# A planned attention and gated-MLP kernel on one core: sharing the three-bank set between ScalarE and VectorE, gating the down projection's halves from PSUM, and recounting the last pass's narrow matmuls

## The chip, the core and the metric

The kernel runs on one NeuronCore of one Trainium2 chip. The metric is device time in microseconds (us) of one execution. A core has five engines with instruction queues of their own: TensorE (PE in the profile; its weight loads are PEld), VectorE (DVE), ScalarE (ACT), GpSimd (POOL) and SyncE (SP). The last two mostly issue DMAs here. PE writes its results to PSUM, which has eight banks of 512 fp32 columns by 128 partitions; ACT and DVE read them there.

## What is computed

The input `x` has 2048 rows (S) of 640 (D) in bf16. A branch of attention (32 heads of 20) and a gated MLP (F = 1728) both read the layer-normed rows; the result is `x + attention * silu(MLP)`.

```python
xn = _layernorm(x)
q, k, v = (xn @ wqkv) ...                        # 32 heads of 20
p = softmax(q @ k.T * 20 ** -0.5)
s = (p @ v).reshape(S, D) @ wo
h = sigmoid(xn @ w_gate) * (xn @ w_up)
g = silu(h @ w_down)
out = x + s * g
```

## The kernel before, in words

**Passes.** After a setup (load, layer norm, transposes, first projections) the work is cut into 32 passes: four chunks of 512 queries (`qc`, QC) times eight groups of four heads (`g`). A pass has 64 score banks: 16 key tiles times four heads, each 128 keys by 512 queries, one PSUM bank. `NB` is 32 x 64 = 2048 banks. The four heads of a group lie on four row strips of PE, so their score matmuls run side by side.

**Exponentials.** ACT takes banks in sets: a set of three banks (`sc0`) and a set of two (`sc1`) in turn, one instruction for a whole set (`act_exp`, L1162). VectorE takes single banks by an approximation in four steps over 512 columns (`dve_exp`: L1173, which is the only one to read PSUM, then L1178, L1182, L1186). Its bank is one of the two work banks (`misc0`, `misc1`), taken as a `spare` by `take_bank` where `spare_wanted` holds one back. `issue` plans one round: it takes the next banks in order, scores them, adds the exponential to ACT's queue and, if VectorE's backlog is under 2500 ns and a work bank is free, a further bank for VectorE. A set is scored again when its `Cell` in `sets` says that it was read.

**Probabilities times values.** `pv_batch` and `pv` (L1274) accumulate eight banks at a time into one bank, `oacc`; row 0 of each head's strip sums the probabilities. After a pass `normalise` copies `oacc` to SBUF (L771), sends the sums through DRAM by GpSimd's DMAs (L772 to L788) and multiplies (L800). The last pass is done in two halves of 256 queries, so that the first half can be finished while the second is still in work: each score bank then holds two key tiles of 256 queries. `first_half` (L806 to L815) copies the first half of `oacc`, `half_job` (L817 to L867) spreads the reciprocals of the sums by two sets of narrow fp32 matmuls (L823, four columns out; L844, 128 columns out) and does the last output matmuls (L862) for row tiles 0 and 1. `part_job` (L750) has summed the first six head groups of the last chunk's output before, times the gate, plus `x` by an accumulating GpSimd DMA (L758).

**The gated MLP.** `gateup_job` makes `hT` (tanh on ACT, L650, reading PSUM; product on VectorE, L660). `down_job` makes one row tile of 640 columns in two halves of 320: 14 matmuls (L679) into a work bank, VectorE copies the half to SBUF (L683), and after both halves ACT takes tanh of the 640 columns from SBUF (L690) and VectorE multiplies (L695). For the last chunk the product stays in SBUF (`gq_last`), for the others it goes to DRAM by a GpSimd DMA (L699). `out_job` (L718, L724) multiplies it into the attention output.

**What sets the order.** The order on every engine is written out while the kernel is built, by a planner that keeps a clock for PE (`pe[0]`) and one each for ACT and VectorE. Its `Engine.run` starts the task that can start first, and by rank among equals. PE's loop (L1351 on) chooses between a round of scores, a batch of probability matmuls, a step of a `Job`, and a zero matmul. Jobs are sorted by a due bank; the last pass's jobs by `NB - 40`, `NB - 16` and `NB - 12`, and at most two jobs are in flight (`runnable`). `zero_add` (L1250 into `oacc`, L1256 into a free work bank) adds a matmul of zeros whenever the planned streaming time of the last 3400 ns (`streamed`, `WINDOW`) is under 2500 (`ENOUGH`). Each matmul enters that count with its planned time: 136 ns for each pick of L823 and 432 for each matmul of L844.

**The end.** After the loop, remaining jobs are emitted, VectorE copies the second half of `oacc` (L1369), the PSUM pool is closed and opened anew, and the same steps follow for row tiles 2 and 3 without the planner: first parts of the output (L1376), picks (L1383), reciprocal (L1388), spread (L1390), fp32 matmuls (L1392), product (L1394), second parts (L1376), `gated` (L871) and `summed` (L874), which also stores.

Of the kernel before, what the change touches and what calls it, by code (L numbers as in the profile page):

```python
# [15 lines left out]
P = 128  # L16
HEAD = 32
GH = 4
# [26 lines left out]
def kernel(  # L45
# [332 lines left out]

    class Engine:
# [286 lines left out]
    def down_job(tt):  # L666
        c, t4 = divmod(tt, QC // P)
        yield "known", lambda: (bulk[0] == NFT and pe[0] > bulk_t[0] + LANDED and len(h_cells.get(c, [])) == NFT and (tt < 2 or tt - 2 in gq_cells)
                                and (c < NQC - 1 or front() >= PER_PASS * (NG * c + t4 + 1)))
        yield "wait", h_cells[c] + ([gq_cells[tt - 2]] if tt > 1 else [])  # L670
        hT = hTs[c]
        d2 = glu[0].tile([P, D], FP32, tag="d2", bufs=2, name="d2")
        got = []
        for h in range(2):
            e0_, e1_ = h * HALF, (h + 1) * HALF
            held, psd = yield "bank",
            for kf in range(NFT):
                fsz = fsz_list[kf]
                nc.tensor.matmul(psd[:, 0:HALF], lhsT=hT[0:fsz, kf, t4 * P:(t4 + 1) * P],  # L679
                                 rhs=glu[1][0:fsz, kf, e0_:e1_], start=(kf == 0), stop=(kf == NFT - 1))  # L680
                yield "mm", MM3
            got.append(dve.add(400.0, [Cell(pe[0] + PE_OUT)], lambda psd=psd, e0_=e0_, e1_=e1_:
                               nc.vector.tensor_copy(out=d2[:, e0_:e1_], in_=psd[:, 0:HALF]), 1))  # L683
            give_bank(held, got[-1])
        d_cells.setdefault(c, []).append(Cell(pe[0]))
        made = {}

        def tanh():
            made["t"] = glu[0].tile([P, D], BF16, tag="td", bufs=1, name="td")
            nc.scalar.activation(out=made["t"], in_=d2, func=ACT.Tanh, scale=0.25)  # L690

        def finish():
            last = c == NQC - 1
            gq = kT_all[:, t4, :].bitcast(FP32)[:, 0:D] if last else d2
            nc.vector.scalar_tensor_tensor(out=gq, in0=made["t"], scalar=1.0, in1=d2, op0=ALU.add, op1=ALU.mult)  # L695
            if last:
                gq_last[t4] = gq
            else:
                nc.gpsimd.dma_start(out=gq_dram[tt, :, :], in_=d2)  # L699

        turned = act.add(590.0, got + td_free[-1:], tanh, 0, EXP_LAG)
        td_free.append(dve.add(740.0, [turned], finish, 2))
        gq_cells[tt] = td_free[-1]

# [101 lines left out]
    half = {}  # L806

    def first_half(done):
        def copy():
            half["oev"] = glu[0].tile([P, KD, P], BF16, tag="wg", bufs=WB, name="oev")  # L810
            half["oev"] = half["oev"].rearrange("p k f -> p (k f)").bitcast(FP32)[:, 0:QH]
            nc.vector.tensor_copy(out=half["oev"], in_=oacc[:, 0:QH])

        cell = dve.add(340.0, [Cell(done + PE_OUT)], copy, -1)
        half["cell"] = cell  # L815
        return cell

    def half_job():
        n, tiles = QH // P, range(QH // P)
        yield "wait", [half["cell"]]  # L820
        held, pd = yield "bank",
        for t4 in tiles:
            nc.tensor.matmul(pd[:, t4 * GH:(t4 + 1) * GH], lhsT=half["oev"][:, t4 * P:(t4 + 1) * P], rhs=pick,  # L823
                             start=True, stop=True, skip_group_check=True)
            yield "mm", MM3
# [6 lines left out]
        def spread():  # L832
            made["rb"] = glu[0].tile([P, KD, P], BF16, tag="wu", bufs=WB, name="rb")
            made["rb"] = made["rb"].rearrange("p k f -> p (k f)").bitcast(FP32)[:, 0:n * P].rearrange(
# [8 lines left out]
        for t4 in tiles:  # L843
            nc.tensor.matmul(prl[:, t4 * P:(t4 + 1) * P], lhsT=made["rb"][:, t4, :, :].rearrange("p j i -> p (j i)"),  # L844
                             rhs=identf, start=True, stop=True, skip_group_check=True)
            yield "mm", 2 * MM5

        def scale():
            oTs[steps[-1]] = wk.tile([P, QC], BF16, tag="oT", bufs=NG + 3, name="oT")
            nc.vector.tensor_tensor(out=oTs[steps[-1]][:, 0:QH], in0=half["oev"], in1=prl[:, 0:QH], op=ALU.mult)  # L850

        cell = dve.add(340.0, [Cell(pe[0] + PE_OUT)], scale, -1)
# [4 lines left out]
        for t4 in tiles:  # L857
# [9 lines left out]
            dve.add(740.0, [out_cells[(NQC - 1) * 4 + t4], *got], lambda t4=t4: summed(t4, pair[:, t4 % 2 * D:(t4 % 2 + 1) * D]), 2)  # L867
# [12 lines left out]
    LAST, QH = NB - PER_PASS, QC // 2  # L880
# [6 lines left out]
    HALF_COST = 12 * MM3 + 4 * MM5  # L887
# [46 lines left out]
    for t4 in range(4):  # L934
        jobs.append(Job(part_job(t4), PART_COST, len(steps) - 1, NB - (40 if t4 < 2 else 16)))
    jobs.append(Job(half_job(), HALF_COST, len(steps) - 1, NB - 12, when=lambda: half))
# [83 lines left out]
    def runnable(p):  # L1020
        k = 0
        while True:
            if k == len(flight):
                if k == MOST:
# [13 lines left out]
    def fill(p, room=1e18):  # L1038
# [4 lines left out]
        pe_do("fill", took)  # L1043
# [24 lines left out]
    NEEDED, NEEDED_LAST = 6, 12  # L1068
# [36 lines left out]
    def dve_bank(banks):  # L1105
# [3 lines left out]
        ends = LAST + PER_PASS // 2 if LAST <= b < LAST + PER_PASS // 2 else PER_PASS * (b // PER_PASS + 1)  # L1109
# [12 lines left out]
    def unit(b):  # L1122
        return b // PER_PASS if b < LAST else len(steps) - 1 + (b - LAST) // (PER_PASS // 2)

    def pieces(b):
        r = b % PER_PASS
        if b < LAST:
            return [(r // GH, 0, 0, QC)]
        half, r = divmod(r, PER_PASS // 2)
        return [(2 * (r // GH) + k, half * QH, k * QH, QH) for k in range(2)]  # L1130

    def full(p):
        return KT if p < len(steps) - 1 else KT // 2
# [62 lines left out]
    def issue():  # L1196
# [6 lines left out]
        if (ci > 1 and dve.backlog + max(0.0, dve.t - pe[0]) < D_BACKLOG  # L1203
                and all(c.t is not None for c in d_made[-2:-1])):
            extra = dve_bank(taken)
            if extra is not None:
                split = take_bank("spare")
        ps = psum.tile([P, n, 512], FP32, tag=f"sc{ci % 2}", bufs=1, name="sc")
# [3 lines left out]
        sets[ci % 2] = act_exp(ps, taken, begun)  # L1212
# [10 lines left out]
    def pv_batch():  # L1223

        p = pv_pass[0]
        if p > len(steps):
# [37 lines left out]
    def pv(batch):  # L1264
# [3 lines left out]
        for k in range(2):  # L1268
            for part in range(1 if p < len(steps) - 1 else 2):
# [18 lines left out]
        if all(n == most for n in pv_count[0]):  # L1288
# [4 lines left out]
            elif p == len(steps) - 1:  # L1293
                oacc_free[0] = first_half(pe[0])
# [10 lines left out]
    while pv_pass[0] <= len(steps):  # L1305
# [47 lines left out]
        if zero_add(room):  # L1353
            idle = False
            continue
        soon = [q[k][1].made.t for q in ready_p for k in range(min(2, len(q)))]
        times = [until, pe[0] + 150.0] + [t + SEM for t in soon if t is not None]
        pe[0] = min(t for t in times if t > pe[0] + 1.0)

    while flight or jobs or timed or act.queue or dve.queue:  # L1360
# [5 lines left out]
    tiles = range(QH // P, QC // P)  # L1366
    units = [(t4, h) for t4 in tiles for h in range(2)]
    oev = wk.tile([P, QC], FP32, tag="oev", bufs=OBUFS, name="oev")
    nc.vector.tensor_copy(out=oev[:, QH:], in_=oacc[:, QH:])  # L1369
# [3 lines left out]
    banks, pd, prl = banks[1:5], banks[6], banks[7]  # L1373
# [6 lines left out]
    for bank, (t4, h) in zip(banks[:3], units):  # L1380
        out_mm(bank, t4, h, NG - 2)
    for k, t4 in enumerate(tiles):
        nc.tensor.matmul(pd[:, k * GH:(k + 1) * GH], lhsT=oev[:, t4 * P:(t4 + 1) * P], rhs=pick,  # L1383
                         start=True, stop=True, skip_group_check=True)
    out_mm(banks[3], *units[3], NG - 2)
# [5 lines left out]
    for k, t4 in enumerate(tiles):  # L1391
        nc.tensor.matmul(prl[:, t4 * P:(t4 + 1) * P], lhsT=rb[:, k, :, :].rearrange("p j i -> p (j i)"), rhs=identf,  # L1392
                         start=True, stop=True, skip_group_check=True)
    nc.vector.tensor_tensor(out=oTs[qc, g][:, QH:], in0=oev[:, QH:], in1=prl[:, QH:], op=ALU.mult)  # L1394
# [34 lines left out]
```

## Time and profile before

| | |
|---|---|
| runs | 898.45, 894.53, 894.62 us; median 894.62 |
| profiled execution | 898.68 us, of which its span (first to last instruction) is 896.5 |
| busy: PE, DVE, ACT, POOL | 809.1, 838.6, 871.4, 161.6 us |
| exponentials on ACT | 717, busy 828.9 us |
| VectorE's first steps (L1173) | 256, 685 ns each |
| mean granted PE clock | 0.99 |

How to read the profile: one execution is recorded. Busy time is the union of an engine's instructions; the mean of one is given in ns. Instructions of an engine overlap at their ends, so the time that one costs is the distance from its start to the next start. "Idle before" is time in which an engine ran nothing, with the instruction whose end released it. The slices cut the span in 40, a digit is the busy share in tenths, and PEclk is the clock that PE was granted, in tenths of full speed. The chain is the work that ended last, followed back.

### The profile page before, as it was taken

How to read it: one execution, taken by the hardware profiler on the slowest of the kernel's cores; microseconds unless marked ns; L12 is line 12 of the kernel's file. 1: busy time of each engine (PE TensorE's matmuls, PEld its weight loads, DVE VectorE, ACT ScalarE, POOL GpSimd, SP SyncE). 2: the span in 40 equal slices, each digit the busy share in tenths (PEclk: the TensorE clock that was granted, in tenths of full speed). 3: DMA queues.
4: the chain of work that ended last, by engine and by line, in shares of the span. 5: the costliest groups of instructions: out<-in, count | busy, mean ns of one | idle time of the engine just before them, and what ended most of it. 6: DMA issues, size and time to landing. Idle time of an engine off the chain costs nothing.

```text
span 896.5 us, 16915 instructions
## 1 busy us (share of the span) xinstructions
PE 809.1 (90%) x6228; PEld 291.8 (33%) x6311; DVE 838.6 (94%) x1483; ACT 871.4 (97%) x837; POOL 161.6 (18%) x305
## 2 busy tenths in 40 slices
PE   5899899998998999999999998999999888999896
PEld 3344333332223333232233332222332322333342
DVE  7799999999999999997999999999999989999994
ACT  6999999999999999999999999999999999999993
POOL 7401111101111212111111221110121220111120
PEclk9999999999999999999999999999999999999996
DMA  8113231235442234223212342303022432200021
GB/s 316 46 36 89 68 105 35 56 94 150 120 122 41 64 89 71 64 58 79 56 25 79 95 65 65 78 24 79 27 73 64 107 64 67 56 20 14 14 59 45
DMA packets 107672, 64.40 MB, mean 72 GB/s; under 512 B 80350, under 2 KB 101906, under 8 KB 107498
## 3 DMA queue, kind: packets, MB, share of 16 engines
q1 hardware_dynamic: 97382, 47.21, 19.8%
q0 software_dynamic: 10208, 16.11, 8.0%
q8 instruction: 49, 0.80, 0.4%
q14 instruction: 33, 0.27, 0.1%
HBM read 50.45 MB, written 16.13 MB: 74 GB/s over the span
## 4 chain that ended last, share of the span: by engine, by line
ACT 63%; issue 18%; PE 11%; DVE 7%; DMA 1%; SPq 0%; ACTq 0%; DVEq 0%
ACT p L1162 58%; PE sc L1140 4%; ACT tnh L650 3%; PE oacc L1274 2%; DVE dy L1173 1%; PE work L643 1%; PE work L123 1%; DVE du L1178 1%; PE work L679 1%; ACT td L690 1%; DVE stats L226 1%; DVE p L1186 1%; DVE du L1182 1%; PE work L149 1%; DMA x_sb<-in_A_x_dram 0%
## 5 line engine op out<-in xcount | busy, mean ns | idle before, releaser
L1162 ACT ACTIVATE p<-sc 128x1536 bf16<-128x1536 f32 x717 | 828.9, 1361 | 3.4 <-PE oacc L1274 1.4
L1140 PE MATMUL sc<-qT,kT_all 21*128 21x512 bf16 (+1 forms) x1850 | 280.9, 377 | 56.5 <-ACT p L1162 48.5
L1173 DVE TENSOR_SCALAR dy<-spare 128x512 f32<-128x512 f32 x256 | 175.2, 685 | 22.6 <-PE spare L1140 20.0
L1140 PEld LDWEIGHTS <-kT_all 21*128 21x128 bf16 x2112 | 90.9, 91 | 286.8 <-issue 275.1
L1182 DVE SCALAR_TENSOR_TENSOR du<-du,dy 128x512 f32<-128x512 f32 x256 | 174.1, 683 | 1.6
L1186 DVE SCALAR_TENSOR_TENSOR p<-du,dy 128x512 uint16<-128x512 f32 x256 | 174.0, 682 | 1.3
L1178 DVE SCALAR_TENSOR_TENSOR du<-dy 128x512 f32<-128x512 uint16 x256 | 174.2, 684 | 0.8
L1274 PE MATMUL oacc<-p,v_all 128*21 128x512 bf16 (+1 forms) x2112 | 158.3, 379 | 0.6 <-DVE v_all L156 0.3
L1140 PE MATMUL spare<-qT,kT_all 21*128 21x512 bf16 (+1 forms) x262 | 98.2, 379 | 0.0
L772 POOL DMA_DIRECT2D den_dram<-oev x31 | 17.9, 578 | 392.8 <-DVE oev L771 392.8
L679 PE MATMUL work<-wd,hT 128*128 128x320 bf16 x448 | 85.5, 302 | 0.1
L643 PE MATMUL work<-xnT,wg 128*128 128x512 bf16 (+1 forms) x261 | 77.6, 383 | 2.0 <-issue 0.6
L656 PE MATMUL work<-xnT,wu 128*128 128x512 bf16 (+1 forms) x268 | 73.1, 381 | 1.2 <-DVE dy L1173 0.3
L788 POOL DMA_DIRECT2D rl<-rec_dram x124 | 61.5, 502 | 57.6 <-DMA rec_dram<-den 47.8
L1250 PE MATMUL oacc<-xnT,zero 128*128 128x512 bf16 x169 | 57.9, 391 | 3.7 <-issue 2.9
L1274 PEld LDWEIGHTS <-v_all 128*21 128x21 bf16 x2112 | 31.4, 90 | 62.9 <-issue 60.7
L679 PEld LDWEIGHTS <-hT 128*128 128x128 bf16 x448 | 35.0, 97 | 48.7 <-issue 39.1
L650 ACT ACTIVATE tnh<-work 128x512 bf16<-128x512 f32 (+1 forms) x56 | 41.4, 738 | 0.0
L660 DVE SCALAR_TENSOR_TENSOR hT<-tnh,work 128x512 bf16<-128x512 bf16 (+1 forms) x56 | 38.0, 679 | 2.2 <-ACT tnh L650 1.9
L782 POOL DMA_DIRECT2D rec_dram<-den x31 | 16.9, 546 | 119.9 <-DVE den L781 115.4
L718 PE MATMUL work<-wo_pad,oT 128*128 128x320 bf16 x192 | 35.5, 302 | 0.5 <-issue 0.5
L643 PEld LDWEIGHTS <-wg 128*128 128x128 bf16 (+1 forms) x280 | 21.7, 98 | 42.8 <-issue 31.1
(122 smaller groups left out, 554.9 us busy)
## 6 DMA issues: line engine op xcount, KB each, us to landing
wg<-in_B_w_gate_dram SPq DMA_DIRECT2D x52, 160.0 KB
wu<-in_B_w_up_dram SPq DMA_DIRECT2D x52, 160.0 KB
rl<-rec_dram POOLq DMA_DIRECT2D x124, 64.0 KB, 2.4
qT<-q_dram SPq DMA_DIRECT2D x31, 128.0 KB
gq_dram<-d POOLq DMA_DIRECT2D x12, 320.0 KB, 2.5
gqr<-gq_dram SPq DMA_DIRECT2D x12, 320.0 KB
kT_all<-k_dram SPq DMA_DIRECT2D x28, 128.0 KB
wd<-in_B_w_down_dram SPq DMA_DIRECT2D x13, 160.0 KB
```

The costliest lines, as they stand in the source:

```text
L643: nc.tensor.matmul(psg[0:fsz, :], lhsT=wg[:, kd, 0:fsz], rhs=xnT[:, kd, cols], start=(kd == 0), stop=(kd == KD - 1))
L650: nc.scalar.activation(out=made["t"][0:fsz, :], in_=psg[0:fsz, :], func=ACT.Tanh, scale=0.5)
L656: nc.tensor.matmul(psu[0:fsz, :], lhsT=wu[:, kd, 0:fsz], rhs=xnT[:, kd, cols], start=(kd == 0), stop=(kd == KD - 1))
L679: nc.tensor.matmul(psd[:, 0:HALF], lhsT=hT[0:fsz, kf, t4 * P:(t4 + 1) * P], rhs=glu[1][0:fsz, kf, e0_:e1_], start=(kf == 0), stop=(kf == N ...
L788: nc.gpsimd.dma_start(out=t["rl"][32 * j:32 * j + 32, :], in_=rec_dram[n, j:j + 1, :].to_broadcast([32, QC]))
L1140: nc.tensor.matmul(ps[:, c0:c0 + n], lhsT=kT_all[rows, g, kt * P:(kt + 1) * P], rhs=qTs[qc, g][rows, q0:q0 + n], start=True, stop=True, ti ...
L1162: nc.scalar.activation(out=buf.tile(), in_=ps, func=ACT.Exp, bias=EXP_BIAS, scale=exp_scale)
L1173: nc.vector.tensor_scalar(out=t["y"], in0=ps, scalar1=LEAST, scalar2=None, op0=ALU.max)
L1178: nc.vector.scalar_tensor_tensor(out=t["u"], in0=t["f"], scalar=CUBE_2, in1=t["f"], op0=ALU.add, op1=ALU.mult)
L1182: nc.vector.scalar_tensor_tensor(out=t["u"], in0=t["u"], scalar=CUBE_1, in1=t["f"], op0=ALU.add, op1=ALU.mult)
L1186: nc.vector.scalar_tensor_tensor(out=buf.tile()[:, 0, :].bitcast(U16), in0=t["u"], scalar=CUBE_SCALE, in1=t["y"], op0=ALU.mult, op1=ALU.add)
L1274: nc.tensor.matmul(oacc[32 * j:32 * j + 1 + Dh, q0:q0 + width], lhsT=v_all[:, kt, GH * g + j, 0:1 + Dh], rhs=buf.ap[:, i, c0:c0 + width], ...
```

## The change

Four things change.

1. In a round of the three-bank set, if VectorE's backlog is under 1300 ns and no work bank was taken as spare, the set's third bank may go to VectorE. ACT's instruction then covers two banks, and the set counts as read when both have read it (`Both`).
2. `down_job` no longer copies its halves: ACT takes tanh of each half of 320 from the work bank, VectorE multiplies it with the same bank, and the bank is given back after that.
3. The last pass is described by `PARTS` (still two of 256). Its jobs get due banks by part: the partial outputs of row tiles 0 and 1 by the end of the first part, those of 2 and 3 by the end of the second. The jobs that finish a part go ahead of others once they can run. The narrow matmuls are counted as 250 ns with no streaming and 330 ns with 200 of streaming, and zero matmuls past the last score are not planned into the time before the next probabilities.
4. At the end, the sum and store of row tile 1 are issued behind the picks of the second part, and two zero matmuls into an unused bank stand before the fp32 matmuls and two behind.

Some buffers change their tag (`oev`, `rb` use `gqr` in place of `wg`, `wu`). The core of the diff:

```diff
     def down_job(tt):
...
+        def tanh(h, psd):
+            made[h] = glu[0].tile([P, HALF], BF16, tag="td", bufs=2, name="td")
+            nc.scalar.activation(out=made[h], in_=psd[:, 0:HALF], func=ACT.Tanh, scale=0.25)
+
+        def gate(h, psd):
...
+            nc.vector.scalar_tensor_tensor(out=made["gq"][:, h * HALF:(h + 1) * HALF], in0=made[h], scalar=1.0,
+                                           in1=psd[:, 0:HALF], op0=ALU.add, op1=ALU.mult)
...
-            got.append(dve.add(400.0, [Cell(pe[0] + PE_OUT)], lambda psd=psd, e0_=e0_, e1_=e1_:
-                               nc.vector.tensor_copy(out=d2[:, e0_:e1_], in_=psd[:, 0:HALF]), 1))
-            give_bank(held, got[-1])
+            turned = act.add(320.0, [Cell(pe[0] + PE_OUT + 100.0), *td_free[-2:-1]], lambda h=h, psd=psd: tanh(h, psd), 0, EXP_LAG)
+            td_free.append(dve.add(400.0, [turned], lambda h=h, psd=psd: gate(h, psd), 1))
+            give_bank(held, td_free[-1])
...
-        turned = act.add(590.0, got + td_free[-1:], tanh, 0, EXP_LAG)
-        td_free.append(dve.add(740.0, [turned], finish, 2))
...
     def last_job(u):
...
-            yield "mm", MM3
+            yield "mm", 250.0, 0.0
...
-            yield "mm", 2 * MM5
+            yield "mm", 330.0, 200.0
...
-            dve.add(740.0, [out_cells[(NQC - 1) * 4 + t4], *got], lambda t4=t4: summed(t4, pair[:, t4 % 2 * D:(t4 % 2 + 1) * D]), 2)
+            end = lambda t4=t4: summed(t4, pair[:, t4 % 2 * D:(t4 % 2 + 1) * D])
+            if u == len(PARTS) - 2 and t4 == tiles[-1]:
+                later.append(end)
+            else:
+                dve.add(740.0, [out_cells[(NQC - 1) * 4 + t4], *got], end, 2)
...
+    PART_DUE = [next(e for e, (q0, width) in zip(ENDS, PARTS) if q0 + width > t4 * P) - 8 for t4 in range(4)]
+    LAST_DUE = [e - 12 for e in ENDS[1:]]
...
     def runnable(p):
+        for x in [x for x in jobs if x.when is not None and x.when()]:
+            jobs.remove(x)
+            flight.insert(sum(y.when is not None for y in flight), x)
...
     def issue():
...
+        shared = None
+        if (not split and n == 3 and ci > 1 and dve.backlog + max(0.0, dve.t - pe[0]) < SHARE
+                and all(c.t is not None for c in d_made[-2:-1]) and dve_bank(taken[:2]) == taken[2]):
+            shared = taken.pop()
...
-        sets[ci % 2] = act_exp(ps, taken, begun)
+        sets[ci % 2] = act_exp(ps[:, 0:len(taken), :] if shared is not None else ps, taken, begun)
+        if shared is not None:
+            score(ps[:, 2, :], shared)
+            issued(shared)
+            sets[ci % 2] = Both(sets[ci % 2], dve_exp(ps[:, 2, :], shared, begun))
...
-        if zero_add(room):
+        soon = [q[k][1].made.t for q in ready_p for k in range(min(2, len(q)))]
+        due = min([t for t in soon if t is not None], default=pe[0]) if b0 >= NB else 1e18
+        if zero_add(min(room, due - pe[0] - MM5)):
...
+    def keep_clock(n):
+        for _ in range(n):
+            nc.tensor.matmul(unused, lhsT=zero, rhs=xnT[:, 0, 0:512], start=True, stop=True, skip_group_check=True)
...
+    for end in later:
+        end()
-    out_mm(banks[3], *units[3], NG - 2)
+    out_mm(banks[-1], *units[-1], NG - 2)
+    keep_clock(2)
```

## The prediction

> **What bounds it now.** First the page: busy shares, slices and the chain that ended last.
>
> ```profile
> PE 809.1 (90%) x6228; PEld 291.8 (33%) x6311; DVE 838.6 (94%) x1483; ACT 871.4 (97%) x837; POOL 161.6 (18%) x305
> ACT  6999999999999999999999999999999999999993
> PEclk9999999999999999999999999999999999999996
> ACT 63%; issue 18%; PE 11%; DVE 7%; DMA 1%; SPq 0%; ACTq 0%; DVEq 0%
> ```
>
> ScalarE (ACT) is full from the second slice to the last but one; VectorE (DVE) has little room, TensorE (PE) a tenth. The last slice is different: ACT is at 3 tenths and the granted clock at 6. So the body is priced by what ACT does per bank, and the end by itself.
>
> Next the groups with shapes apart, then ACT's timeline, whose starts give what one instruction really costs, since their spans overlap.
>
> ```profile
> L1162 ACT ACTIVATE p<-sc 128x1536 bf16<-128x1536 f32 x358 | 563.9, 1575 | 1.0 <-PE sc L1140 0.6 <-PE spare L1140 0.4
> L1162 ACT ACTIVATE p<-sc 128x1024 bf16<-128x1024 f32 x359 | 411.9, 1147 | 2.4 <-PE oacc L1274 1.4 <-PE sc L1140 0.7
> L690 ACT ACTIVATE td<-d 128x640 bf16<-128x640 f32 x16 | 13.0, 812 | 0.6 <-ACT p L1162 0.3 <-DVE d L683 0.2
> ```
>
> ```profile
> 213.14 0.69 ACT L650 ACTIVATE tnh<-work 128x512 bf16<-128x512 f32 x1
> 213.61 6.08 ACT L1162 ACTIVATE p<-sc 128x1536 bf16<-128x1536 f32 x5
> 219.41 0.77 ACT L650 ACTIVATE tnh<-work 128x512 bf16<-128x512 f32 x1
> ...
> 312.67 3.88 ACT L1162 ACTIVATE p<-sc 128x1536 bf16<-128x1536 f32 x3
> 316.78 0.74 ACT L690 ACTIVATE td<-d 128x640 bf16<-128x640 f32 x1 [0.23 <-DVE d L683]
> ```
>
> A line merges the alternating widths under its first. From start to next start the median is 1.330 us after a width of 1536, 0.904 after 1024, 0.477 after 512: the five from 213.61 to 219.41 take 3 x 1.330 + 2 x 0.904 = 5.80, as shown. That is 0.832 ns a column plus 0.05. Whatever exceeds these steps is ACT waiting: 9.7 us from 60 to 876 us, in pieces mostly under 0.3. The wait ahead of td at 316.78 is 0.54 (the three before it need 3.57, and took 4.11); td at 324.60, 646.67 and 680.35 waited 0.48, 0.11 and 0.47 likewise.
>
> Last the end, by windows (columns: window, length, then PE, PEld, DVE, ACT and POOL busy, granted clock, DMA) and by the timeline.
>
> ```profile
> 872.65:876.06 3.41, 3.04 (x46) 1.94 (x42) 2.78 (x8) 3.41 (x4) 0.91 (x1) 1.00 0.19 52
> 876.06:879.50 3.44, 3.44 (x34) 1.25 (x32) 1.53 (x4) 2.81 (x4) 0.00 (x0) 0.50 0.41 94
> 882.90:886.30 3.40, 3.31 (x21) 1.13 (x21) 0.02 (x1) 0.82 (x1) 0.00 (x0) 0.50 0.12 40
> ```
>
> ```profile
> 882.69 1.02 ACT L1162 ACTIVATE p<-sc 128x1024 bf16<-128x1024 f32 x1 [0.48 <-PE sc L1140]
> ...
> 882.92 2.34 PE L1250 MATMUL oacc<-xnT,zero 128*128 128x512 bf16 x5 [0.33 <-issue]
> ...
> 885.19 1.04 PE L1274 MATMUL oacc<-p,v_all 128*21 128x256 bf16 x16
> 886.28 0.42 DVE L1369 COPY oev<-oacc 128x256 f32<-128x256 f32 x1 [4.35 <-PE oacc L1274]
> 886.76 0.57 PE L1376 MATMUL last<-wo_pad,oT 128*128 128x320 bf16 x3 [0.53 <-DVE oev L1369]
> ...
> 887.76 0.21 DVE L1388 RECIPROCAL rq<-last 128x8 f32<-128x8 f32 x1 [1.06 <-PE last L1383]
> ```
>
> From 876.06 to 886.30 the clock is halved, although PE was busy 3.04 of the 3.41 us before. Counting columns at full speed (overlapping row tiles once) I get 0.42 of that window as streaming; the least of any window from 60 to 870 us is 0.51. The narrow fp32 matmuls of L823 and L844 stand in it: eight records, few columns. So dense but narrow work seems to lose the clock.
>
> The Trainium skill ("TensorE: Matmul & The Clock Gate", "Why this matters for your kernels") asks only for no PE-idle gaps over about 3 us; this row shows a fall without one, and I go by the row.
>
> **What the fall costs, and which runs had it.** After 876 ACT waits 2.0 us beyond its steps. Its last exponential ends at 883.71, but five zero matmuls at 0.47 hold the queue and the last probability matmuls end at 886.23: 2.5 later, where 0.55 would do at full clock (eight of the sixteen, 0.3, and release 0.25). Together 4.0. The profiled execution took 898.7 (span 896.5 and 2.2 around it), the runs 898.45, 894.53, 894.62: two levels 4 us apart. I take the lower level, the median's, for executions without the fall.
>
> **The change, step by step.** Counts are from the two kernels' instruction order.
>
> *Exponentials.* Width 1536: 358 to 341; 1024: 359 to 379; one of 512. VectorE's chains: 256 to 266, 19 of them from the set's third bank, nine fewer from a spare. ACT: -17 x 1.330 + 20 x 0.904 + 0.477 = **-4.0 us**. All is on the bounding engine.
>
> *VectorE* pays 10 x 4 x 0.60 = 24.0 (its steps, start to start); it drops 32 copies of 0.40 and 16 gates of 0.73 for 32 half gates, whose nearest row is the 320-wide product from PSUM (L724, 0.40): net +12.3. Its windows from 60 to 860 us hold 35 us of idle time, so this is covered; if that cover failed, up to 12.3 would show.
>
> *The set's wait.* A shared set waits for VectorE's first step too, and the scores of the round after next stand behind it on PE. The spare chains show 0.34 to 1.39 us from score to first step (median 0.55), which itself lasts 0.69; ACT's own exponential ends about 1.65 after the score. So each costs 0 to 0.43, 19 at most 8 us; no earlier release is in it beyond the shorter exponential already counted. I take 0: only 2% start later than 1.2.
>
> *Halved tanh.* By columns 0.317 each, 0.634 a pair against 0.633 now; by the 512 row 0.954. So 0 to +5.1 for 16; I take 0, as three widths lie on one line. The wait for VectorE's copy goes: **-1.6**. Next due is PE's own last matmul, and the tnh row, which waits so, shows 0.0 idle. The bank is held until the gate, some 2 us more, which is why spares fall. The gate waits for tanh with VectorE's chains behind it; the same pattern at L660 idles 1.9 us in 56.
>
> *Narrow matmuls counted right.* A zero matmul now stands before the picks and one after the fp32 products; by columns the last pass comes to 0.50 to 0.66. I take the fall as gone: **-4.0** against the profiled execution, nothing against the lower level. Outside, 21 fewer zeros are issued (220 to 199), off ACT's path.
>
> *The end, paid back.* The partial products of row tiles 2 and 3 are due later, and one group of six is issued after the last probability matmul, with four of the first part's last. Count from e, ACT's end. VectorE has two gated halves, a partial half and a sum (0.83) queued ahead of the accumulator's copy, the last done at e+1.25; copy 0.35, first gate 0.40: e+2.0 frees a bank; six matmuls of 0.15 and 0.25 out: e+3.2; their half gate 0.48: e+3.7. The ending's first matmul waits for the last reader of PSUM, as 886.76 waited for the copy; the reciprocal is 1.0 later (886.76 to 887.76): e+4.75. Now, at full clock, it is 0.55 + 1.53 = e+2.1. **+2.7**, with 0 (cover by an earlier bank) and +4 (half clock in it) as bounds. Moved with it is GpSimd's accumulating DMA, 3.8 us to landing: issued at about e+3.9, landed by e+8.6; its reader, the last sum, starts at e+9.5. The earlier sum's store moves on SP's queue but is not last. The four zero matmuls beside reciprocal and spread (887.76 to 888.35) take 0.43 a pair at full clock: hidden; at half, up to +0.5 a pair.
>
> **Sum.** From the profiled execution: 898.7 - 4.0 - 1.6 - 4.0 + 2.7 = 891.8. From the median: 894.6 - 4.0 - 1.6 + 2.7 = 891.7. I forecast **891.8**, with 889 to 894 as its own range: 1.5 either way for waits of a replanned order, and a half clock at the end.
>
> **Rivals.**
> - *All of it shows* (0.34). The 4 us between the levels are something else, the median runs had the fall too: 894.6 - 6.9 = 887.7; or the end is not paid back: 889.0. For it: one profile cannot say which level has the fall. Against: 4.0 fits the gap.
> - *The clock falls anyway* (0.12): 891.8 + 4.0 = 895.8. For it: 0.50 lies between 0.42, which fell, and 0.51, which did not. By the Trainium skill's rule above this case would have no chance, since PE never idles so long.
> - *Slower* (0.10): the third bank binds ACT to VectorE. It decides once a shared round loses more than 0.39 us on average (7.3 / 19), that is, if VectorE's first step begins near the longest start seen; at 0.43 it gives 900. Against: the median of 0.55.
>
> **The numbers.** Forecast 0.44, of which 0.08 lies below 890.1. Faster by over 0.5% (under 890.1; about what a measurement of this kernel can tell from no change): 0.34 + 0.08 = 0.42. Within: 0.36 + 0.12 = 0.48. Slower (over 899.1): 0.10. The range 887.5 to 896.5 holds the first three cases.
>
> **What would show it.** ACT's steps 1.330, 0.904, 0.317 with 341 + 379 + 1 exponentials; td waiting for nothing; clock 1.00 until the last exponential; the reciprocal 4 to 5 us after that, behind the late partial half. Wrong it is if ACT's waits ahead of three-bank rounds grow by more than 2 us, if the clock falls in the body, or if runs of the kernel before without the fall are not 4 us shorter.

## The result, and the profile after

The changed kernel takes **909.44 us** (median of 906.53, 907.67, 911.21 and 913.89) where the kernel before took 896.46 beside it (median of 894.53, 894.62, 898.31 and 898.45). The ratio on record is 1.0157, with a 95% interval of 1.0130 to 1.0184; the two medians alone give 1.0145, since the one before falls between two levels. It is slower by about 1.5%; 891.8 was forecast. The profiled execution took 913.9, of which the span is 912.0.

From the page of the changed kernel: busy shares, slices, the chain that ended last.

```profile
PE 811.7 (89%) x6212; PEld 291.7 (32%) x6294; DVE 851.1 (93%) x1507; ACT 871.4 (96%) x857; POOL 162.0 (18%) x305
ACT  6999999999989999999999999999999999999992
PEclk9999999999979999999999999999999999999988
ACT 49%; issue 17%; DVE 16%; PE 16%; DMA 2%; POOL 0%; SPq 0%; DVEq 0%; ACTq 0%; POOLq 0%
```

ScalarE is busy for as long as before, but in a longer span. Two marks are new: one slice in the body (the twelfth) in which the clock falls, and a chain in which VectorE has 16% where it had 7%. Next the groups with shapes apart and the waits of ScalarE and VectorE (columns of the waits: who waited for what, us in total, times, longest).

```profile
L1184 ACT ACTIVATE p<-sc 128x1536 bf16<-128x1536 f32 x341 | 522.9, 1533 | 5.1 <-PE sc L1162 3.7 <-PE spare L1162 1.3
L1184 ACT ACTIVATE p<-sc 128x1024 bf16<-128x1024 f32 x379 | 413.8, 1105 | 11.1 <-PE sc L1162 5.1 <-DVE dy L1195 4.0 <-PE oacc L1304 1.4
L686 ACT ACTIVATE td<-work 128x320 bf16<-128x320 f32 x32 | 17.2, 538 | 0.0
```

```profile
ACT p L1184 <- PE sc L1162: 8.8, 19, 1.4
ACT p L1184 <- DVE dy L1195: 4.0, 8, 1.6
```

```profile
DVE dy L1195 <- ACT p L1184: 9.5, 9, 1.4
```

The counts are the forecast ones, and td waits for nothing. But ScalarE waits for the scores of its sets, and for VectorE's first step (`dy`), and that step waits for ScalarE's exponential. No data passes between these two: they read different banks of one set, and the set is one tile of the program. The timeline shows both kinds. First a set that ScalarE reads first:

```profile
208.02 2.94 ACT L1184 ACTIVATE p<-sc 128x1024 bf16<-128x1024 f32 x3
...
208.37 0.39 PE L1162 MATMUL sc<-qT,kT_all 21*128 21x512 bf16 x3
...
210.08 0.69 DVE L1195 TENSOR_SCALAR dy<-sc 128x512 f32<-128x512 f32 x1 [1.19 <-ACT p L1184]
...
210.82 0.39 PE L1162 MATMUL sc<-qT,kT_all 21*128 21x512 bf16 x3 [1.20 <-DVE dy L1195]
...
211.25 1.45 ACT L1184 ACTIVATE p<-sc 128x1536 bf16<-128x1536 f32 x1 [0.30 <-PE spare L1162]
```

The shared set is scored at 208.37; ScalarE's exponential of its two banks ends at 210.05; only then does VectorE start, 1.71 us behind the scores. The next scores of the set stand at 210.82, behind VectorE's step, and ScalarE, done with the set between, starts 0.53 late at 211.25. In the second kind VectorE is first:

```profile
261.12 0.68 DVE L1195 TENSOR_SCALAR dy<-sc 128x512 f32<-128x512 f32 x1
...
261.90 3.28 ACT L1184 ACTIVATE p<-sc 128x1024 bf16<-128x1024 f32 x3 [0.50 <-DVE dy L1195]
```

ScalarE, free before, starts as VectorE's step ends. All 19 shared sets are of these kinds: in nine VectorE starts 0.03 us after ScalarE's end (1.66 to 2.31 us behind the first of the set's scores), in ten ScalarE starts 0.77 to 0.79 us after VectorE's start. ScalarE's waits around them (to about 5 us behind VectorE's step, those in a fallen clock included) come to 14.2 us. Then the clock (columns as in the prediction's windows):

```profile
259.43:262.84 3.41, 2.35 (x25) 0.69 (x25) 3.15 (x6) 2.91 (x5) 1.41 (x3) 1.00 0.83 224
262.84:266.25 3.41, 3.28 (x10) 0.79 (x9) 2.69 (x5) 2.34 (x3) 0.00 (x0) 0.50 0.14 45
...
269.67:273.08 3.41, 3.41 (x18) 0.76 (x16) 2.89 (x5) 3.01 (x3) 0.00 (x0) 0.50 0.32 75
273.08:276.49 3.41, 3.41 (x25) 0.91 (x23) 2.61 (x5) 3.27 (x5) 0.00 (x0) 1.00 0.22 48
```

In the window of the set at 261.12 PE was busy for 2.35 us, and the clock is halved for the next 10.24. It falls again at 805.56 for 3.41 and at 884.07 for 6.83. Last the end:

```profile
897.47 0.42 DVE L822 COPY oev<-oacc 128x256 f32<-128x256 f32 x1
...
898.33 0.97 PE L758 MATMUL work<-wo_pad,oT 128*128 128x320 bf16 x6 [0.90 <-DVE kT_all L886]
899.34 0.49 DVE L763 SCALAR_TENSOR_TENSOR hT<-work,kT_all 128x320 f32<-128x320 f32 x1 [0.67 <-PE work L758]
...
900.14 0.87 POOL L766 DMA_DIRECT2D hT<-in_A_x_dram  x1 [7.79 <-DVE hT L763]
...
900.89 0.21 DVE L1427 RECIPROCAL rq<-last 128x8 f32<-128x8 f32 x1 [0.33 <-PE last L1419]
```

The last exponential ends at 896.36, the reciprocal starts 4.53 later, after the late group of six (L758). The last VectorE operation ends at 906.47 and the last store has landed at 907.92, but the span ends at 912.0.

**Where the 15.5 us between the two profiled spans come from:** the first exponential 0.3 later; from there to the end of the last one 12.3 more, though ScalarE's steps there are 3.5 shorter (833.0 against 836.5); to the reciprocal 0.5; to VectorE's end nothing; behind that 2.4.

### The profile page after: what moved, and what is told of

It is laid out like the page before. It is cut to its first block, busy times and chain, and to the rows that moved or that the text cites. A ratio compares the mean times of both kernels' runs of the same rounds, so it can differ in the third digit from the quotient of the medians.

```text
span 912.0 us, 16855 instructions
## 1 busy us (share of the span) xinstructions
PE 811.7 (89%) x6212; PEld 291.7 (32%) x6294; DVE 851.1 (93%) x1507; ACT 871.4 (96%) x857; POOL 162.0 (18%) x305
## 4 chain that ended last, share of the span: by engine, by line
ACT 49%; issue 17%; DVE 16%; PE 16%; DMA 2%; POOL 0%; SPq 0%; DVEq 0%; ACTq 0%; POOLq 0%
ACT p L1184 45%; PE sc L1162 5%; DVE dy L1195 4%; DVE du L1200 3%; DVE du L1204 3%; DVE p L1208 2%; PE oacc L1304 2%; ACT tnh L659 2%; PE work L704 2%; PE work L665 2%; PE work L652 2%; PE work L124 1%; ACT td L686 1%; DVE stats L227 1%; DMA gqr<-gq_dram 1%
## 5 line engine op out<-in xcount | busy, mean ns | idle before, releaser
L1184 ACT ACTIVATE p<-sc 128x1536 bf16<-128x1536 f32 (+2 forms) x721 | 828.7, 1307 | 16.2 <-PE sc L1162 8.8
L1162 PE MATMUL sc<-qT,kT_all 21*128 21x512 bf16 (+1 forms) x1857 | 283.8, 379 | 62.0 <-ACT p L1184 47.5
L1204 DVE SCALAR_TENSOR_TENSOR du<-du,dy 128x512 f32<-128x512 f32 x266 | 180.4, 682 | 1.9
L1208 DVE SCALAR_TENSOR_TENSOR p<-du,dy 128x512 uint16<-128x512 f32 x266 | 180.3, 681 | 1.6
L1200 DVE SCALAR_TENSOR_TENSOR du<-dy 128x512 f32<-128x512 uint16 x266 | 180.3, 682 | 1.0
L1195 DVE TENSOR_SCALAR dy<-spare 128x512 f32<-128x512 f32 x247 | 168.3, 682 | 13.7 <-PE spare L1162 12.3
L1162 PE MATMUL spare<-qT,kT_all 21*128 21x512 bf16 (+1 forms) x255 | 95.0, 378 | 0.7 <-DVE gqr L732 0.7
L1280 PE MATMUL oacc<-xnT,zero 128*128 128x512 bf16 x152 | 51.5, 386 | 2.7 <-issue 2.1
L659 ACT ACTIVATE tnh<-work 128x512 bf16<-128x512 f32 (+1 forms) x56 | 37.7, 674 | 0.1
L665 PEld LDWEIGHTS <-wu 128*128 128x128 bf16 (+1 forms) x280 | 24.0, 98 | 40.7 <-issue 24.6
```

The source lines that it names most:

```text
L659: nc.scalar.activation(out=made["t"][0:fsz, :], in_=psg[0:fsz, :], func=ACT.Tanh, scale=0.5)
L665: nc.tensor.matmul(psu[0:fsz, :], lhsT=wu[:, kd, 0:fsz], rhs=xnT[:, kd, cols], start=(kd == 0), stop=(kd == KD - 1))
L1162: nc.tensor.matmul(ps[:, c0:c0 + n], lhsT=kT_all[rows, g, kt * P:(kt + 1) * P], rhs=qTs[qc, g][rows, q0:q0 + n], start=True, stop=True, ti ...
L1184: nc.scalar.activation(out=buf.tile(), in_=ps, func=ACT.Exp, bias=EXP_BIAS, scale=exp_scale)
L1195: nc.vector.tensor_scalar(out=t["y"], in0=ps, scalar1=LEAST, scalar2=None, op0=ALU.max)
L1200: nc.vector.scalar_tensor_tensor(out=t["u"], in0=t["f"], scalar=CUBE_2, in1=t["f"], op0=ALU.add, op1=ALU.mult)
```

## The experiments

Theory A: of the two readers of a shared set, the one that is later in the program waits for the other, and this makes the loss. Its rivals look for it elsewhere in the change. All times are medians; "before" ran beside each on the same chip at 894.8 to 895.1.

**Without shared sets.**

```diff
-    NEEDED, NEEDED_LAST, SHARE = 6, 12, 1300.0
+    NEEDED, NEEDED_LAST, SHARE = 6, 12, -1.0
```

> The whole change but the sharing of the third bank (its backlog limit set below zero): 358 and 359 exponentials again, 256 VectorE chains, all from spares. Theory A (in a shared round one of the two readers waits for the other: VectorE's first step starts when ScalarE's exponential of the same set ends, or the exponential when VectorE's step ends, about 0.5 us of ScalarE lost each time, and PE, which starves meanwhile, loses its clock): the loss goes; 890 to 896 us, ScalarE waiting about as long from 60 to 876 us as in the kernel before less 1.6. Theory B (the work banks held until the half gates make PE's jobs late): stays near 905 or above. Theory C (fewer zero matmuls and the recount let the clock fall): stays near 905 or above, clock falls in the body.

Measured: 894.92 us, ratio to before 1.0006 (0.9988 to 1.0024). The loss is gone with the shared sets alone, so it isn't in the other edits. Nor is there a gain.

**Shared sets without the mutual wait.** The order stays as it is. One declaration tells the framework that the two instructions don't depend on each other, which is so: each reads its own banks, and neither writes them.

```diff
+    def both_read(key, made):
+        other = readers.setdefault(key, made.ins)
+        if other is not made.ins:
+            tc.declare_no_dep(made.ins, other, reason="they read different banks of the set")
...
-            nc.scalar.activation(out=buf.tile(), in_=ps, func=ACT.Exp, bias=EXP_BIAS, scale=exp_scale)
+            made = nc.scalar.activation(out=buf.tile(), in_=ps, func=ACT.Exp, bias=EXP_BIAS, scale=exp_scale)
+            if key is not None:
+                both_read(key, made)
```

(and the same in `dve_exp`).

> The whole change with the same instructions in the same order, but the two readers of a shared set, which read different banks, are declared independent of each other, so that neither waits for the other; the scores of the next round on the set still wait for both. Theory A: the 0.4 to 0.6 us after each of the 19 shared rounds go, and with them the falls of the clock that follow them: 888 to 893 us, VectorE's first step 0.35 to 0.6 us after its score throughout. If the wait of the next scores for VectorE's step is what costs, and not the order of the two readers: 900 or more, waits of three-bank rounds remain. Theories B and C: 905 or more.

Measured: 897.57 us, ratio 1.0027 (1.0013 to 1.0042), between the ranges that were given. The set that was scored at 208.37 above, in this kernel's timeline:

```profile
207.63 4.29 ACT L1191 ACTIVATE p<-sc 128x1024 bf16<-128x1024 f32 x4
...
207.99 0.39 PE L1162 MATMUL sc<-qT,kT_all 21*128 21x512 bf16 x3
...
208.43 0.69 DVE L1204 TENSOR_SCALAR dy<-sc 128x512 f32<-128x512 f32 x1
```

VectorE starts 0.44 us behind the scores, beside ScalarE, and ScalarE runs on. Over the 19 sets ScalarE waits 1.4 us where it waited 14.2, and VectorE starts 0.44 to 1.08 behind the scores. **11.9 us of the loss go with the mutual wait**, 0.62 for each set, the falls of the clock that follow it included. The Trainium skill ("Advanced Engine Details and Errata", "Bank Collisions") says that ScalarE and VectorE read PSUM at the same time at full bandwidth if their banks differ; the trace agrees, with VectorE's step at 685 ns beside ScalarE here and 686 from a spare. It was a dependence that the framework keeps, not the memory, that held them apart: the instructions and their order are the same here. But 2.7 us against the kernel without shared sets stay, where A expected a gain: something else in sharing costs.

**One part alone, from the kernel before:** shared sets (first), the halves gated from PSUM (second), and the last pass recounted, with its end (third, the changed kernel with the other two taken out).

```diff
+        if (not split and n == 3 and ci > 1 and dve.backlog + max(0.0, dve.t - pe[0]) < SHARE
+                and all(c.t is not None for c in d_made[-2:-1]) and dve_bank(taken[:2]) == taken[2]):
+            shared = taken.pop()
```

> The kernel before with the sharing alone: 343 and 378 exponentials, 263 chains, 17 of them shared; copies, whole gates and the last pass as before. Theory A: slower than the kernel before by 17 x 0.5 = 8 us and more where the clock falls: 904 to 912. Theories B and C: within 3 us of the kernel before, or faster by the 2.8 us of exponentials saved.

Measured: 906.40 us (901.21 to 914.42), ratio 1.0125 (1.0088 to 1.0162): sharing alone makes most of the loss.

```diff
-            got.append(dve.add(400.0, [Cell(pe[0] + PE_OUT)], lambda psd=psd, e0_=e0_, e1_=e1_:
-                               nc.vector.tensor_copy(out=d2[:, e0_:e1_], in_=psd[:, 0:HALF]), 1))
+            turned = act.add(320.0, [Cell(pe[0] + PE_OUT + 100.0), *td_free[-2:-1]], lambda h=h, psd=psd: tanh(h, psd), 0, EXP_LAG)
```

> The kernel before with the halves gated straight from PSUM alone: 32 tanh of 320 columns from the work banks, no copies. Theory A: the 1.6 us that tanh waited for VectorE's copies go and nothing else changes: 892 to 897. Theory B: slower than the kernel before by 5 us or more, PE's job matmuls waiting for work banks. Theory C: as A.

Measured: 899.51 us, ratio 1.0045 (1.0026 to 1.0064): slower, a miss. Its last exponential ends at 881.62 and the reciprocal starts 6.4 us later. The replanned order puts eight of the first part's output matmuls behind the last probability matmuls; their gates and sums hold VectorE until 885.80, and the accumulator's copy waits there. With the recount (the first kernel above) the reciprocal follows after 1.96. So is the recount worth 4.6 us?

> The kernel before with the last pass's recount alone (parts, due times, zero matmuls by the narrow count, and the end's zero matmuls), the down projection's halves and the sets as before. The gated halves without the recount took 899.5 us, and with it 894.9. If what the recount brings adds up, this is 894.8 - 4.6 = about 890 (889 to 892). The rival: the recount only puts right what the gated halves had moved at the end, and this kernel is within 1 us of the kernel before (894 to 896).

Measured: 894.52 us, ratio 0.9988 (0.9977 to 0.9999). The rival holds: the recount puts right what the halves had moved at the end, and is worth less than 1 us by itself. And the halves bring nothing: from the first exponential to the last one's start it is 849.8 us here and 849.9 with them.

**The late part of the end.** What is left of sharing was sought there. The edit moves the order at the end only: no shared set in the last 128 banks before the last pass, with and without the mutual wait.

```diff
-        if (not split and n == 3 and ci > 1 and dve.backlog + max(0.0, dve.t - pe[0]) < SHARE
+        if (not split and n == 3 and ci > 1 and at_bank[0] < LAST - 128 and dve.backlog + max(0.0, dve.t - pe[0]) < SHARE
```

> The changed kernel without the mutual wait of the two readers, and with no shared set in the last 128 banks before the last pass (18 shared sets in place of 19). Its order at the end is other: the last part of the output projection (line 758) stands ahead of the last scores, not behind the last exponentials. Theory A (what was left of the loss, 2.7 us against the kernel without shared sets, is the late part: reciprocal 4.5 us behind the last exponential in place of 2.0, and the end of the span held by GpSimd's drain 11.1 us behind the part's DMA): last exponential over at 879.6, reciprocal at 881.6, last VectorE operation over at 887.2, span 890.8, time 891 to 893.5. Rival: sharing itself costs what is left, wherever it is put: 896 to 898.

Measured: **891.84 us**, ratio 0.9962 (0.9949 to 0.9975). This is the kernel that is faster than both. Its end:

```profile
871.23 0.92 POOL L766 DMA_DIRECT2D hT<-in_A_x_dram  x1 [2.05 <-DVE hT L763]
...
878.08 0.83 PE L1315 MATMUL oacc<-p,v_all 128*21 128x256 bf16 x16
...
881.32 0.21 DVE L1438 RECIPROCAL rq<-last 128x8 f32<-128x8 f32 x1 [0.20 <-PE last L1430]
```

The last part's DMA is issued at 871.23, before the last scores, not behind the last exponential (over at 878.48); the reciprocal follows it after 2.84, and the span ends 3.1 behind VectorE's last operation. Against the kernel with the late part the profiled span is 4.8 shorter: exponentials 0.7, reciprocal 1.7, and 2.4 at the very end.

> The changed kernel, mutual wait and all, with no shared set in the last 128 banks before the last pass. Theory A: the late part of the end goes with its 2.5 + 1.9 us, the mutual wait stays: 904 to 907, against 909.4 of the changed kernel. Rival: the end is late because of the mutual wait, and the time stays at 908 to 912.

Measured: 902.58 us, ratio 1.0088 (1.0070 to 1.0107). It gains 6.9 where 2 to 5 were expected. Part of that is the clock: one fall of 3.41 us stands in its profile, where the changed kernel's had three. Between the fastest executions of both, at granted clocks of 0.998 and 0.997, the gain is 4.8. The mutual wait is the rest of the distance to 891.84: 10.7 us for 18 sets.

**Is it GpSimd's drain?** Without shared sets, one small DMA behind the last reciprocal:

```diff
     nc.vector.reciprocal(out=rq.rearrange("p t j -> p (t j)"), in_=pd[:, 0:GH * n])
+    nc.gpsimd.dma_start(out=rec_dram[0, 0:2, :].rearrange("j (r c) -> (j r) c", c=GH * QC // P // 2), in_=rq.rearrange("p t j -> p (t j)"))
```

> The changed kernel without shared sets, and one small GpSimd DMA more (4 KB of the last reciprocals, into memory that nothing reads any more), issued right behind the last reciprocal. Theory A (GpSimd's drain lasts 11.1 us from its last DMA's issue whatever the DMA is): issue at about 883.7, drain over at 894.8, span about 895.5, 3 us more than without it (897 to 898.5 against 894.9). Rival (the drain ends when the DMA has landed, some 2 us behind its issue): no change, 894 to 896.

Measured: 898.31 us, 3.4 more than without it. From its timeline:

```profile
886.36 0.57 POOL L1428 DMA_DIRECT2D rec_dram<-rq  x1 [5.65 <-DVE rq L1427]
...
890.59 0.82 DVE L889 TENSOR_TENSOR ot<-kT_all,hT 128x640 bf16<-128x640 f32 x1
```

Its span is 898.4: 12.1 behind the issue of that DMA, and 7.0 behind VectorE's end, where it is 3.6 without the DMA. The record of GpSimd's drain lasts 10.87 us here and 11.09 in the changed kernel, from the last DMA's issue, for 4 KB and for 320 KB. Theory A holds; the DMA itself had landed by 888.06.

**The dose.** A looser limit shares 31 sets, with and without the mutual wait.

```diff
-    NEEDED, NEEDED_LAST, SHARE = 6, 12, 1300.0
+    NEEDED, NEEDED_LAST, SHARE = 6, 12, 2200.0
```

> The changed kernel with the mutual wait, no shared set in the last 128 banks before the last pass, and a looser limit (2200 in place of 1300), so that 31 sets are shared in place of 18; the exponentials' steps come to the same sum (796.4 us against 797.0). In the kernel with 18 ScalarE waited 11.2 us around them, 0.62 us for each. Theory A (each shared set costs its mutual wait): 13 more cost 8 us, 909 to 913 against 902.6. Rival (a few rounds, or the clock, made most of the loss): 902 to 905.

Measured: 920.91 us, ratio 1.0275 (1.0238 to 1.0311). The loss grows with the number of sets, by more than was expected: from the first exponential to the last one's start it is 26.8 us longer than in its twin without the wait, 0.86 a set (10.8 for 18 sets, 0.60). Its profile has four falls of the clock before the end. Without most of these it is still more: the fastest executions of the two kernels, at granted clocks of 0.998 and 0.999, lie 22.4 us apart, 0.72 a set.

> The same 31 shared sets without the mutual wait. In the kernel with 18 ScalarE waited 1.3 us around them, and the exponentials' steps come to the same sum here. Theory A: 890.5 to 893, as with 18 (891.8). Rival (shared sets cost something without the wait too, such as VectorE's work in front of the other steps): 894 or more.

Measured: 896.70 us, ratio 1.0016 (1.0001 to 1.0030). The rival's time holds: from the first exponential to the last one's start it is 851.8 us, against 846.8 with 18 sets, and ScalarE's waits around the sets are 5.2 us, not 1.3. Why isn't shown. VectorE isn't shorter of room: from 60 to 860 us it idles 25.5 us here and 23.7 with 18 sets. Of ScalarE's longest waits in the body, one (1.2 us, to 736.13) stands behind scores that waited for VectorE, which had waited for a DMA; another (1.0, to 199.81) behind gate weights that landed late.

**What the clock takes.** Two runs tried to fill PE's waits with zero matmuls: by a higher mark in the planner, and by three matmuls in each shared round.

```diff
-    WINDOW, ENOUGH = 3400.0, 2500.0
+    WINDOW, ENOUGH = 3400.0, 2700.0
```

> The changed kernel with a higher mark for its zero matmuls (2700 in place of 2500 ns in a window): 302 in place of 199, the same 19 shared sets, the late part of the end as before. In the changed kernel's profile ScalarE waited 7.0 us while the clock was at half or just after. Theory: these waits are the falls' and go with them, 903 to 906 against 909.4. Rival: they are the mutual waits' whatever the clock, and the time stays at 908 to 912.

Measured: 918.08 us, ratio 1.0239 (1.0204 to 1.0274): neither answer. The whole order was replanned, and a gate weight was asked for late:

```profile
193.68:197.10 3.42, 2.34 (x20) 0.71 (x17) 3.42 (x8) 3.42 (x4) 0.02 (x1) 1.00 0.14 43
197.10:200.51 3.41, 0.81 (x4) 0.30 (x5) 0.09 (x1) 0.86 (x1) 0.56 (x1) 1.00 1.00 219
200.51:203.92 3.41, 3.41 (x11) 0.66 (x9) 2.21 (x7) 1.81 (x2) 0.57 (x1) 0.50 0.27 62
```

PE waited 3.5 us for that load (its waits name `wg<-in_B_w_gate_dram`), all engines stood, and the clock was halved for 17.07 us. As a price of the falls it tells nothing.

```diff
         if shared is not None:
+            for _ in range(3):
+                nc.tensor.matmul(ps[:, 2, :], lhsT=zero, rhs=xnT[:, 0, 0:512], start=True, stop=True, skip_group_check=True)
             score(ps[:, 2, :], shared)
```

> The changed kernel, its order as it is, with three zero matmuls more in each of the 19 shared rounds, ahead of the third bank's scores and into that bank, which the scores then overwrite: TensorE streams while the two readers wait for each other. In all nine records with a fall of the clock inside the passes, the 3.41 us window before it had TensorE busy for less than any neighbour (0.8 to 2.7 us in eight). Theory A (some 5 of the changed kernel's 14.7 us are falls that follow such windows): the falls at the shared rounds go, the direct waits of 0.5 to 0.8 us a set stay, 902 to 906. Rival (the waits alone make the loss, and falls come whatever TensorE does): no faster than the changed kernel, 907 to 913.

Measured: 923.33 us, ratio 1.0349 (1.0310 to 1.0388), against 909.14 for the changed kernel on the same chip. It is neither range. In the profiled execution, at a clock of 0.997, no fall is left before 914 us of its span, but three of the six executions had 0.982 to 0.990, so falls weren't ruled out. And the zeros cost more than the falls, as the profiled execution, free of these, took 921.02:

```profile
207.82 0.39 PE L1162 MATMUL sc<-qT,kT_all 21*128 21x512 bf16 x2
208.14 0.82 PE L1241 MATMUL sc<-xnT,zero 128*128 128x512 bf16 x3
208.90 0.38 PE L1162 MATMUL sc<-qT,kT_all 21*128 21x512 bf16 x1
...
209.38 1.94 ACT L1184 ACTIVATE p<-sc 128x1024 bf16<-128x1024 f32 x2 [0.80 <-PE sc L1162]
```

ScalarE reads only the two banks scored at 207.82, yet it starts behind the scores of the third, at 208.90: it waits for the whole tile's writers too. ScalarE's waits around the sets rise from 14.2 to 26.2 us.

> The changed kernel itself, timed again beside the one with zeros in its shared rounds on the same chip: 907 to 913, as before (median 909.4 of 906.5 to 913.9).

Measured: 909.14 us, ratio 1.0163 (1.0150 to 1.0176). Its profile gives a price of the falls: the same program with 6.83 us of half clock before its last exponential, not 20.48, has that exponential's start 4.9 us sooner behind the first one.

The granted clock that is on record for every execution separates waits and falls better. The fastest execution of the changed kernel took 906.53 us at 0.997; without the wait the two at 0.997 took 895.60 and 895.78. With 18 sets the three with the wait at 0.998 or 0.999 took 901.74 to 902.28, those without it, all at such a clock, a median of 891.84. That is 10.8 and 10.2 us, 0.57 a set both times. The changed kernel's other executions lie up to 7.4 higher, at clocks down to 0.987. **Some 10 to 11 us of the loss are direct waits, and the falls that follow them add 0 to 7**, different from run to run. As an estimate from these runs the loss adds up: 10.8 of waits, 2.9 of falls (the median over the fastest), 4.1 of the late part, less 3.1 of shorter exponentials, make 14.7 of 14.8 (909.4 against 894.6).

**Do the halves matter in the faster kernel?** The down projection as before, 17 shared sets:

```diff
-            turned = act.add(320.0, [Cell(pe[0] + PE_OUT + 100.0), *td_free[-2:-1]], lambda h=h, psd=psd: tanh(h, psd), 0, EXP_LAG)
+            got.append(dve.add(400.0, [Cell(pe[0] + PE_OUT)], lambda psd=psd, e0_=e0_, e1_=e1_:
+                               nc.vector.tensor_copy(out=d2[:, e0_:e1_], in_=psd[:, 0:HALF]), 1))
```

> The kernel that was faster than both (shared sets without the mutual wait, none in the last 128 banks before the last pass, narrow matmuls recounted), with the down projection gated in one piece from a copy, as in the kernel before: 17 shared sets. Theory: the halves bring nothing that can be measured, as they brought nothing without shared sets (894.9 with them, 894.5 without): 891 to 893. Rival: they bring their 1.6 us of waits for VectorE's copies, and the time is 893 to 895.

Measured: 893.89 us (891.84 to 898.29), ratio 0.9990 (0.9970 to 1.0010). Unclear: its profiled execution, of 892.27, has the exponentials' stretch at 846.9 us against 846.8 with the halves, so nothing there. The median lies in the rival's range, but its executions go with the granted clock: six of 891.84 to 894.24 at 0.996 to 0.998, four of 895.79 to 898.29 at 0.990 to 0.995. Why the clock falls in so many of them, and with the halves in none of six (0.998 and 0.999), wasn't found.

## Why the prediction was wrong, step by step

- **Exponentials, -4.0: right in kind.** Counts and steps came as forecast. Without the wait, 18 sets shorten the stretch from first to last exponential from 849.9 to 846.8, by 3.1 of the 3.2 that the steps give.
- **VectorE, +12.3, covered: right.** It was busy 12.5 us longer, and without the wait ScalarE loses 1.4 around the sets. With 31 sets it loses 5.2, from a cause that stays open.
- **The set's wait, taken as 0, at most 0.43 a set: the step that failed.** The bound came from the spare chains, whose first step starts 0.34 to 1.39 us behind the scores. But a spare has one reader. In a set with two readers the framework kept them in program order, so VectorE started where ScalarE ended, at 1.66 or later, or ScalarE waited for VectorE, which no row of the spares could show. The price was 0.62 a set, 11.9 us by the medians, of which 0.57 a set is the wait itself and the rest the falls behind it. The slower rival named the place and the point from which it decides (0.39), but gave it 0.10, and looked for a late VectorE, not for an order between readers.
- **Halved tanh, -1.6: wrong size, it measured nothing.** The tanh of a half takes the forecast 0.317 us and td waits for nothing, but the exponentials' stretch is the same with and without the halves (849.9 and 849.8); where ScalarE waits in its place wasn't found.
- **Narrow matmuls, the fall: the level was right, "the fall as gone" isn't shown.** 75 executions of the kernel before ran beside the experiments. 65 of them took 894.5 to 895.5 us at a granted clock of 0.996 to 0.999, ten took 898.5 to 899.0 at 0.990 to 0.993; the profiled one, with the fall, had 0.990. So the lower level is the one without the fall, 4 us shorter as forecast, and the premise of the rival "all of it shows", that the median runs had it too, is wrong. But the recount didn't end such falls. In 13 profiles of kernels with it the clock fell at 869 to 897 us in five; without shared sets the same order kept the clock in one profile and lost it at 872.10 in that with the late DMA. With the halves alone, without the recount, it stayed up to the last exponential. The 0.50 of streaming counted on was no safe mark (last section). The prediction's other sign, a fall in the body, came with the mutual waits.
- **The end, +2.7: right, but a term was missing.** The reciprocal came 4.53 us after the last exponential (4.75 forecast) for the reason given. The GpSimd DMA that moves with the late part was called harmless, since it lands before its reader. Its drain was not in the sum: +2.4 on the span.

With the wait and the late part taken out, the change takes 891.84 us, within 0.1 of the forecast. This is partly luck: of its terms, -1.6 did not come, and the reciprocal's delay there is 2.84 us, not 4.75, so two misses cancel.

## What to carry to other kernels

Giving one bank of a shared tile to a second engine adds two edges, not one: the tile waits for both readers, and the readers may be ordered among themselves. Look for a consumer's idle time that ends with the other consumer's end, and tell the framework where no order is needed. Note the granted clock of every execution: it told here which executions of one kernel held a fall. When a step moves towards the end, price the queue that it leaves behind to its last drain, and not only to its reader.

## What the runs showed of the hardware

- **GpSimd's drain at the end lasts about 11 us from its last DMA's issue:** 10.87 to 11.31 us in all 16 profiles. It costs nothing if that DMA is old enough (the faster kernel's span ends 18.8 us behind it); in the changed kernel the span ended 11.86 us behind it.
- **The clock falls without an idle PE.** In the windows of 3.41 us before the 18 falls inside the passes of ten profiles, PE was busy 0.8 to 3.0 us. The Trainium skill ("TensorE: Matmul & The Clock Gate", "Why this matters for your kernels") asks for no gap over about 3 us. One fall agrees with it, behind the wait of 3.51 us for a gate weight; the other 17 came with a longest gap of 0.3 to 1.4 us. Low busy time is no rule either: the changed kernel kept its clock after a window with 2.22 us of it (to 211.6) and lost it after one with 2.35. Falls last one, two, three or five windows.
- **The columns streamed tell more than busy time.** Counted as in the prediction (columns at full speed, overlapping row tiles once), the window before each of the 18 falls held 0.15 to 0.52 of streaming. In all 16 profiles, from 60 us to the last exponential, ten windows at full clock held under 0.43, and the clock fell behind every one. Of 53 with 0.43 to 0.52 it fell behind eight, and of some 3,790 with more behind none. So the prediction's bound of 0.51, taken from one profile, was too low. This is a count over these runs; no run set the streaming alone.
